# A four-stage transformer kernel: gate/up as pairs of 64-row tiles, down products in batches of their own, transposes by DMA

## The chip, the cores and the metric

One core of one Trainium2 chip. The metric is the device time of one execution in microseconds; lower is better. The kernel before takes 1253.09 us (median of the 4 runs made beside the changed kernel).

## The reference

Two layers, each a linear attention block with softmax feature maps and then a gated product (GLU), with residuals. S = 2048 tokens, D = 576, 32 heads of 18, F = 4608, bf16. Both layers use the same weights.

```python
qkv = x @ wqkv                                   # q, k, v per head
pq, pk = q @ w_phi, k @ w_phi                    # per head, 18 x 18
phi_q = concat([softmax(pq), softmax(-pq)]);  phi_k = likewise
kv = phi_k^T v;  z = sum over tokens of phi_k
attn = (phi_q kv) / (phi_q z + 1e-6) @ wo
glu  = ((x @ w_gate) * (x @ w_up)) @ w_down      # no nonlinearity
x = x + attn(layernorm(x)); x = x + glu(layernorm(x)); x = x + attn(layernorm(x)); x = x + glu(layernorm(x))
```

All K and V of a layer must be done before its first Q can be finished (kv is a sum over all tokens). That makes two places in which little else can run: the start, and the middle between the layers.

## The kernel before

The program is written as Python threads (`t_load`, `t_ln`, `t_ain` for K and V, `t_aout` for Q, `t_bmain` for the GLU, `t_wd` for the ring of down weights). A list scheduler orders their operations by modelled durations and emits one instruction stream per engine. The order is thus itself a product of the change: moving one operation can reorder others.

In the GLU, the 576 rows of the contraction are four full K tiles of 128 and one of 64. Gate and up each take five matmuls per step of 128 of the 4608 columns, the fifth with a zero half; the down product of a step follows two steps later, so both kinds interleave all through.

```python
for k in range(5):                       # gate
    lhsT = Wg[:, k, fs] if k < 4 else Wr[:, fs]
    ops.append(... matmul(ps[:, gub, 0:256], lhsT, xT[:, k, tok], ...))
for k in range(5):                       # up; the half row is read from xT[:, 5]
    lhsT = Wu[:, k, fs] if k < 4 else Wr[:, fs]
    ops.append(... matmul(ps[:, gub, 256:512], lhsT, xT[:, k if k < 4 else 5, tok], ...))
...                                      # two steps later: 2 x (512 + 64) columns of the down product
    ps[:, bank, 0:512] += hT . wdr[:, slot, fi, 0:512];  ps[:, Z, ...] += hT . wdr[:, slot, fi, 512:576]
```

The gate, up and attention weights stay on chip. The down weights (5.3 MB) do not fit and are streamed again for every block of 256 tokens, through a ring of three slots of 432 KB (`NWD = 3`, `CH = 3`: three steps to a piece). Every load is issued from SyncE. The layer norm's output is transposed on TensorE:

```python
ops.append(Op(60, lambda e: e.transpose(pT[:, 128*k:128*k+128], xln[:, sl[j], 128*k:128*k+128], s.ident[:])))
... act: copy(xT[:, 0:5, tok], pT)
```

## Time and profile before

| | before |
|---|---|
| median | 1253.09 us (1250.22 to 1254.75) |
| PE busy, share of span | 96% |
| first gate matmul | 125.25 us |
| one GLU step, gate/up and down | 1.09 + 0.49 us |
| down weights | 192 pieces of 432 KB, 3.3 us to land (median) |

How to read it: a PE at 96% leaves only PE work and the two attention-bound places to gain from.

### The profile page before, as it was taken

Reading aid. Unit: us, or ns where it says so; the run is one execution under the profiler, and the core shown is the slowest. Engines: PE = TensorE matmul, PEld = TensorE weight load, DVE = VectorE, ACT = ScalarE, POOL = GpSimd, SP = SyncE. Lnnn points to the kernel's source line nnn. Section 1 sums busy time; section 2 is a strip of 40 time slices with the busy share of each in tenths; the row PEclk is TensorE's granted clock in tenths of the full one; section 3 lists DMA queues with packets and bytes.
Section 4 is the critical chain, followed back from the end, with each engine's and each line's share of the span. In section 5 each row is a group of like instructions: output and inputs, shape, how many; then the busy total and the mean of one; then the engine's idle time right before and its main releaser. Section 6 shows DMA issues by size and latency. Waiting matters only on the chain.

```text
span 1250.4 us, 25739 instructions
## 1 busy us (share of the span) xinstructions
PE 1198.8 (96%) x11096; PEld 936.1 (75%) x11096; DVE 619.3 (50%) x1478; ACT 546.4 (44%) x1393; POOL 272.5 (22%) x268
## 2 busy tenths in 40 slices
PE   6796999999999999999999889999999999999998
PEld 4574777778787777777767568778777777777776
DVE  6898646445553323323269974455445332323232
ACT  7887545445353323222258765444444322222222
POOL 4796212112120000000039742112112000000000
PEclk9998999999999999999999889999999999999999
DMA  9700122222222333333320002222222233323232
GB/s 316 230 2 1 41 75 72 74 85 72 85 73 86 88 99 89 98 90 97 94 64 2 1 2 73 86 82 74 82 84 82 86 97 99 105 91 110 87 109 67
DMA packets 85832, 104.61 MB, mean 84 GB/s; under 512 B 4374, under 2 KB 84566, under 8 KB 84566
## 3 DMA queue, kind: packets, MB, share of 16 engines
q1 hardware_dynamic: 85718, 102.96, 27.0%
q8 instruction: 87, 1.43, 0.5%
q14 instruction: 27, 0.22, 0.1%
HBM read 100.59 MB, written 2.36 MB: 82 GB/s over the span
## 4 chain that ended last, share of the span: by engine, by line
PE 84%; DVE 6%; POOL 5%; ACT 4%; issue 0%; DMA 0%; SPq 0%; DVEq 0%
PE ps L1071 25%; PE ps L1076 25%; PE ps L1109 20%; PE ps L808 4%; PE ps L1019 3%; POOL dd L869 3%; PE ps L1112 3%; DVE ss L855 2%; PE ps L946 2%; POOL dd L833 1%; PE ps L965 1%; PE ps L783 1%; DVE dd L841 1%; PE ps L998 1%; DVE mxmn L823 1%; DVE mxmn L828 1%
## 5 line engine op out<-in xcount | busy, mean ns | idle before, releaser
L1086 DVE TENSOR_TENSOR hT<-ps,gsb 128x256 bf16<-128x256 f32 x576 | 243.9, 423 | 577.2 <-ACT gsb L1084 575.9
L1084 ACT CAST gsb<-ps 128x256 bf16<-128x256 f32 x576 | 214.2, 372 | 621.7 <-PE ps L1076 585.3
L1109 PE MATMUL ps<-wdr,hT 128*128 128x512 bf16 x1152 | 357.5, 379 | 0.4 <-DVE x_sb L1135 0.4
L1071 PE MATMUL ps<-xT,Wg 128*128 128x256 bf16 x2304 | 347.2, 273 | 0.0
L1076 PE MATMUL ps<-xT,Wu 128*128 128x256 bf16 x2304 | 346.1, 273 | 0.0
L1071 PEld LDWEIGHTS ps<-xT,Wg 128*128 128x128 bf16 x2304 | 187.2, 98 | 80.8
L1076 PEld LDWEIGHTS ps<-xT,Wu 128*128 128x128 bf16 x2304 | 225.7, 98 | 26.4
L1112 PE MATMUL ps<-wdr,hT 128*128 128x64 bf16 x1152 | 221.9, 193 | 0.5 <-DVE x_sb L1138 0.5
L869 POOL TENSOR_TENSOR dd<-dd,rr 128x576 bf16<-128x576 bf16 x128 | 146.1, 1163 | 121.1 <-ACT rr L863 121.1
L1109 PEld LDWEIGHTS ps<-wdr,hT 128*128 128x128 bf16 x1152 | 112.6, 98 | 76.8 <-DVE x_sb L1135 0.7
L1071 PE MATMUL ps<-xT,Wr 128*128 128x256 bf16 x576 | 157.2, 273 | 0.0
L1076 PE MATMUL ps<-xT,Wr 128*128 128x256 bf16 x576 | 157.2, 273 | 0.0
L772 POOL TENSOR_SCALAR xln<-x_sb,nmean,rstd 128x576 bf16<-128x576 bf16 x64 | 51.9, 821 | 367.1 <-ACT rstd L767 366.9
L833 POOL TENSOR_TENSOR dd<-psb,mxmn 128x576 bf16<-128x576 bf16 x64 | 74.4, 1163 | 231.6 <-DVE mxmn L823 231.6
L1112 PEld LDWEIGHTS ps<-wdr,hT 128*128 128x128 bf16 x1152 | 112.7, 98 | 6.5 <-DVE x_sb L1138 0.8
L855 DVE TENSOR_REDUCE ss<-dd 128x64 f32<-128x1152 bf16 x64 | 86.4, 1350 | 22.8 <-ACT dd L850 22.5
L1071 PEld LDWEIGHTS ps<-xT,Wr 128*128 128x128 bf16 x576 | 56.5, 98 | 6.6
L1076 PEld LDWEIGHTS ps<-xT,Wr 128*128 128x128 bf16 x576 | 56.4, 98 | 6.6
L820 ACT CAST psb<-ps 128x288 bf16<-128x288 f32 x128 | 47.9, 400 | 17.3 <-PE ps L808 15.3
L949 ACT COPY eT<-ps 108x768 bf16<-108x768 bf16 x64 | 50.8, 798 | 8.5 <-PE ps L965 4.9
L828 DVE TENSOR_REDUCE mxmn<-ps 128x16 f32<-128x288 f32 x128 | 52.0, 448 | 0.0
L841 DVE TENSOR_TENSOR dd<-ps,mxmn 128x288 bf16<-128x288 f32 x128 | 51.7, 447 | 0.0
(85 smaller groups left out, 1143.8 us busy)
## 6 DMA issues: line engine op xcount, KB each, us to landing
wdr<-in_B_w_down_dram SPq DMA_DIRECT2D x192, 432.0 KB, 3.3
Wg<-in_B_w_gate_dram SPq DMA_DIRECT2D x4, 1152.0 KB, 12.3
Wu<-in_B_w_up_dram SPq DMA_DIRECT2D x4, 1152.0 KB, 27.3
x_sb<-in_A_x_dram SPq DMA_DIRECT2D x4, 576.0 KB, 5.8
out_dram<-x_sb SPq DMA_DIRECT2D x8, 288.0 KB, 3.7
Wraw<-in_A_wqkv_dram SPq DMA_DIRECT2D x8, 144.0 KB, 4.8
Wv<-in_A_wqkv_dram SPq DMA_DIRECT2D x1, 576.0 KB, 3.9
Wo<-in_A_wo_dram SPq DMA_DIRECT2D x1, 576.0 KB, 6.6
```

What stands on the lines that cost most here:

```text
L772: ops.append(Op(800, (lambda e, j=j: e.tensor_scalar(xln[:, sl[j], 0:576], x_sb[:, ss[j], :], nm[:, sl[j]:sl[j] + 1], rstd[:, sl[j]:sl[j] ...
L828: ops.append(Op(370, (lambda e, h=h, pv=pv: e.tensor_reduce(mxmn[:, pz, 1, 16 * h:16 * h + 16], pv, AX.X, ALU.min)), reads=[("pbd", bank)] ...
L833: yield ("ops", "pool", [Op(1170, (lambda e: e.tensor_tensor(d1, p3, mxb, ALU.subtract)), reads=[("psb", pz, 0), ("psb", pz, 1), ("mx", pz ...
L841: ops.append(Op(370, (lambda e, d2h=d2h, pv=pv, mnbh=mnbh: e.tensor_tensor(d2h, pv, mnbh, ALU.subtract)), reads=[("pbd", bank), ("mn", pz, ...
L855: Op(1320, (lambda e: e.tensor_reduce(ss[:, sm, :].rearrange("p (b g) -> p b g", b=2), e4, AX.X, ALU.add)), reads=s.ddk(sm, 0) + s.ddk(sm, ...
L869: yield ("ops", "pool", [Op(1150, (lambda e, ev=ev, rb=rb: e.tensor_tensor(ev, ev, rb, ALU.mult)), reads=s.ddk(sm, br) + [("rr", sm), ("dd ...
L1071: ops.append(Op(d_pe(256), (lambda e, lhsT=lhsT, rhs=rhs, k=k, gub=gub: e.matmul(ps[:, gub, 0:256], lhsT, rhs, start=(k == 0), stop=(k == ...
L1076: ops.append(Op(d_pe(256), (lambda e, lhsT=lhsT, rhs=rhs, k=k, gub=gub: e.matmul(ps[:, gub, 256:512], lhsT, rhs, start=(k == 0), stop=(k = ...
L1084: yield ("ops", "act", [Op(372, (lambda e, g=g, gub=gub: e.copy(gsb[:, g, :], ps[:, gub, 0:256])), reads=[("GUg", gub)], writes=[("gsb", g ...
L1086: yield ("ops", "dve", [Op(425, (lambda e, g=g, h=h, gub=gub: e.tensor_tensor(hT[:, h, :], ps[:, gub, 256:512], gsb[:, g, :], ALU.mult)), ...
L1109: ops.append(Op(d_pe(512), (lambda e, lhsT=lhsT, bank=bank, slot=slot, fi=fi, f2=f2: e.matmul(ps[:, bank, 0:512], lhsT, s.wdr[:, slot, fi, ...
L1112: ops.append(Op(d_pe(64) + 6, (lambda e, lhsT=lhsT, sl=sl, slot=slot, fi=fi, f2=f2: e.matmul(ps[:, Z, 64 * sl:64 * sl + 64], lhsT, s.wdr[: ...
```

## The change

Its intent: save the wasted half of the fifth K tile, take the transposes off TensorE, and put work into the idle middle.

* Gate and up run as nine pairs of concurrent 64-row tiles per step. A `lock` keeps attention off TensorE for a gate/up batch of 36 steps (256 tokens).
* Then comes the down batch of those 36 steps, alone but for attention, which shares this phase.
* The K work of layer 2 is done under GLU 1, as far as its tokens are ready.
* Seven heads per attention tile instead of six (five overlapping tiles instead of six).
* The layer norm's output is transposed by DMA. These DMAs and the down weights are issued from SyncE; the loads of all other weights, and of x, move to ScalarE's queue.
* The ring of the down weights is four slots of 288 KB.

```diff
-CH = 3
+CH = 2
-        self.NPS, self.NSM, self.NVX, self.NET, self.NXP, self.NWD = 2, 4, 2, 3, 3, 3
+        self.NPS, self.NSM, self.NVX, self.NET, self.NXP, self.NWD, self.NG, self.NO = 2, 4, 2, 3, 2, 4, 2, 1
 # t_load
-                yield ("dma", g, emit, (), writes, nbytes, False)
+                yield ("dma", g, emit, (), writes, nbytes, False, False, 60.0, "act")
 # t_ln
-            yield ("ops", "pe", [... e.transpose(pT[...], xln[...], s.ident[:]) x 5 ...]) ; act copies
+            yield ("dma", s.g_xt[sl[j]], (lambda e: e.dma_start_transpose(xT[:, :, tok], xln[:, sl[j], :])), ...)
 # GLU (cut to its core)
+        def part(half, W, wk, which, tail):
+            r = slice(64 * half, 64 * half + 64)
+            ...
+                    seq = [(W[r, k, fs], s.xT[r, k, tok]) for k in range(4)]
+                    if tail:
+                        seq.append((s.Wr[r, fs], s.xT[r, 4, tok]))
+        lo = part(0, s.Wg, "Wg", 0, True) + part(0, s.Wu, "Wu", 1, False)
+        hi = part(1, s.Wu, "Wu", 1, True) + part(1, s.Wg, "Wg", 0, False)
+        for a_, b_ in zip(lo, hi):
+            ops += [a_, b_]
 ...
+            yield ("lock",)          # one gate/up batch
+            ...
+            yield ("unlock",)
+            yield ("go", s.t_down(L, b, on_block_done), 4, ...)   # 36 steps of the down product
```

## The prediction

> **What bounds the kernel now.** I read the page's busy row and its 40 slices first, then busy time by stretch, then the timeline of one steady GLU step, then the groups by shape.
>
> ```profile
> PE 1198.8 (96%) x11096; PEld 936.1 (75%) x11096; DVE 619.3 (50%) x1478; ACT 546.4 (44%) x1393; POOL 272.5 (22%) x268
> ...
> PE   6796999999999999999999889999999999999998
> ...
> DVE  6898646445553323323269974455445332323232
> ```
>
> TensorE (PE) is the bound in all but two places: the first four slices and the middle (slices 21 to 24), where VectorE (DVE) is full instead. Those are the attention K stages of layers 1 and 2. The table by stretch (PE, weight loads, DVE, ACT, POOL, granted clock, DMA share, GB/s) shows it:
>
> ```profile
> 0.00:125.00 125.00, 94.88 (x905) 71.12 (x906) 105.39 (x234) 100.46 (x254) 88.49 (x94) 0.95 0.42 137
> ...
> 145.00:640.00 495.00, 495.00 (x4595) 390.44 (x4593) 204.29 (x520) 181.58 (x472) 52.02 (x53) 1.00 0.29 86
> 640.00:732.00 92.00, 78.79 (x714) 57.96 (x713) 85.44 (x170) 74.15 (x188) 75.06 (x68) 0.93 0.02 6
> ...
> 750.00:1246.00 496.00, 494.81 (x4557) 389.20 (x4555) 194.16 (x482) 169.06 (x431) 43.04 (x42) 1.00 0.29 88
> ```
>
> Busy time of overlapped matmuls says little, so I need the distance between starts. One GLU step (128 of the 4608 columns, 256 tokens):
>
> ```profile
> 400.71 0.60 PE L1071 MATMUL ps<-xT,Wg 128*128 128x256 bf16 x4
> 401.15 0.27 PE L1071 MATMUL ps<-xT,Wr 128*128 128x256 bf16 x1
> 401.25 0.60 PE L1076 MATMUL ps<-xT,Wu 128*128 128x256 bf16 x4
> 401.69 0.27 PE L1076 MATMUL ps<-xT,Wr 128*128 128x256 bf16 x1
> 401.80 0.38 PE L1109 MATMUL ps<-wdr,hT 128*128 128x512 bf16 x1
> 402.02 0.19 PE L1112 MATMUL ps<-wdr,hT 128*128 128x64 bf16 x1
> 402.05 0.38 PE L1109 MATMUL ps<-wdr,hT 128*128 128x512 bf16 x1
> ```
>
> Ten 256-column matmuls take 401.80 - 400.71 = 1.09 us, 109 ns each; a 512 plus a 64 of the down product takes 0.245 us, so the down pair 0.49 us. A step is 1.58 us and there are 576, so the GLUs are 910 us of the 1250. In the same way the timeline gives 124 ns per 288-column matmul, 137 per 324, 57.5 per K-V outer product and 51 to 56 per transpose or attention output. Multiplied by the counts, all PE work is: gate/up 5760 x 109 = 628; down 576 x 0.49 = 282; Q, K and output projections 960 x 124 = 119; V 320 x 137 = 44; 864 transposes 48; K-V 22, attention output 20, weight fusion 6: 1169 us. The other 81 us of the span are PE idle or cold, about 45 of them before 125 us, 23 in the middle, the rest at the two ramps and the end.
>
> **What the Trainium skill says.** (1) "TensorEngine Tiling (Array Packing)", Key Properties: row tiles execute weight loads and matmuls in parallel; changing the tiling mode drains TensorE. Its Gotcha 1: two row tiles may not access one PSUM bank at once. The kernel before has no row tiles, so its trace cannot confirm this. The diff keeps the two tiles on different banks and swaps them half way through each group of four steps, with an ordering wait. (2) "TensorE: Matmul & The Clock Gate", Part 3, says that a weight load overlaps matmuls in flight only if its row group differs, and gives 3.07x for four 32-row tiles. The trace is better than the first half:
>
> ```profile
> 400.44 0.10 PEld L1109 LDWEIGHTS ps<-wdr,hT 128*128 128x128 bf16 x1
> 400.46 0.10 PEld L1112 LDWEIGHTS ps<-wdr,hT 128*128 128x128 bf16 x1
> ```
>
> full-array loads start 0.02 us apart while a matmul of the same rows runs. Two loads per 109 ns, which a tile pair needs, therefore look affordable. (3) "DMA: Bandwidth & Descriptors", Rules for kernel authors: transfers from several issuing queues share the same 16 engines. So the loads moved to ACT's queue will still interleave with the new transposes; in the first 50 us the trace has the DMA full (share 0.9 to 1.0).
>
> **The change, part by part.**
>
> *Gate/up.* 576 is 4.5 rows of 128. Before, the half row costs a whole zero-padded matmul for gate and another for up. After, nine 64-row halves of gate and nine of up run as nine concurrent pairs. If a pair costs what one full matmul costs (109), 576 x 9 x 109 = 565: 63 us less.
>
> *LN transposes to DMA.* 320 PE transposes x 56 ns go: 18 us of PE, and about 0.95 us of ACT per 128 tokens. Added: 64 DMA transposes of 160 KB, which lengthen each LN's latency by an estimated 3 us, hidden except in the start and the middle.
>
> *Seven heads per tile.* Per Q tile 10 instead of 12 transposes and outputs, per K tile 10 instead of 12 outer products; V 576 columns instead of 648. V 44 to 39, transposes of attention 30 to 27, K-V 22 to 19, output 20 to 19, fusion 6 to 5: 13 us less.
>
> PE work becomes 1169 - 63 - 18 - 13 = 1075 us. Mode switches: two per 256-token block, 32 in all; a drain is the 273 ns life of a matmul less its 109 ns slot, an estimated 0.16 us, so 5 us.
>
> *Where it is idle.* I rebuild the span by stage.
> (a) Start. DVE and POOL bind the K stage (3.42 us per tile in the timeline from 62 to 97 us), and that work stays. The K stage ended near 97.5; the first gate matmul came at 125 after two Q tiles. The new order lets the first gate/up batch start only when four Q tiles are done; before, the fourth was done near 138 us while sharing with GLU. I take 135.
> (b) GLU 1 from there: gate/up 8 x 35.3 = 282; down 8 x 17.6 = 141; twelve remaining Q tiles at 3.9 (10 x 124 for Q, as many for the output, 15 transposes, 10 outputs) = 47; fourteen K tiles of layer 2 at 3.0 = 42. Sum 512.
> (c) Middle: after the last down batch a serial chain. LN took 8.5 us before (x2 at 640 to xT at 648.5), plus 3 for the DMA; two K tiles 11.5 + 3.5; the K-V add and the barrier 6; then four Q tiles to x1, which took 42 us before (704 to 746) while the GLU had begun, here an estimated 33 alone. Sum 66 us, of which 22 are PE work. Before, 640 to 732 took 92 and the ramp lost 3 more.
> (d) GLU 2: 282 + 141 + 47 = 470. (e) End 5.
> Sum 135 + 512 + 66 + 470 + 5 = 1188; with switches 1193.
>
> *What a batch design can lose besides.* In a gate/up batch the pair of banks needed next must be emptied in 18 slots, 1.96 us; ACT (0.54, from 512 columns) then DVE (0.63), the matmul's tail and semaphores make about 1.6. One attention instruction in between, such as the 1.35 us DVE sum, eats the margin. I take 0.7 us per block, 11 us in all. Total 1204.
>
> ```profile
> L855 DVE TENSOR_REDUCE ss<-dd 128x64 f32<-128x1152 bf16 x64 | 86.4, 1350 | 22.8 <-ACT dd L850 22.5
> L828 DVE TENSOR_REDUCE mxmn<-ps 128x16 f32<-128x288 f32 x128 | 52.0, 448 | 0.0
> L841 DVE TENSOR_TENSOR dd<-ps,mxmn 128x288 bf16<-128x288 f32 x128 | 51.7, 447 | 0.0
> ...
> wdr<-in_B_w_down_dram SPq DMA_DIRECT2D x192, 432.0 KB, 3.3
> ```
>
> **The rivals.**
> R1, *the tiles are not really concurrent*. If half-row weight loads or the bank writes of two tiles collide, a pair could cost 130 to 150 ns instead of 109. Each 10 ns is 52 us. For it: skill's 3.07 of 4. Against it: the two load starts above. At 130 the total is near 1310.
> R2, *attention no longer fits the down phase*. The lock gives PE to gate/up for 35 us, so the two Q tiles of the next block must pass their chain (projection, maxima, exponentials, sums, normalising, transposes, output) within one down phase. Summing the durations of the groups for two tiles gives about 23 us; the phase has 17.6 + 7.8 = 25.4 us of PE work in layer 2, 31.5 in layer 1. For it: 2 us of slack only. If each of the twelve phases that hold Q tiles ran 4 us over, the total would be 1250.
> R3, *the down weights become the bound*. A batch reads 5.3 MB; 1.2 MB are prefetched, leaving 4.1 MB for 17.6 us, 235 GB/s, in phases with no attention, against 86 before. For it: 3.3 us to land a 432 KB piece. Against it: the start moves 316 GB/s, and only the last two blocks of GLU 2 and to a lesser degree of GLU 1 are so bare. About 4 to 8 us.
> R4, *the transposes starve the start*. With the loads full until 50 us, LN could wait for its transposes; the K stage would shift by 5 to 20 us.
>
> **Range and chances.** The stage sum with small losses is 1204. Perfect overlap gives 1193, and a shorter middle or start could take 20 more: 1170. R2 to R4 together, each at half its size, add some 40: 1245. R1 gets about 8%, and alone makes it slower. The 2% line is at 1229.0, a little less than one spread above 1204. I give 0.80 for faster by over 2%, 0.13 within, 0.07 slower.
>
> **What would show each step.** In the profile after: gate/up pairs at 108 to 112 ns from pair start to pair start (R1 if more); a gate/up batch of about 35 us without holes over 0.5 us (eviction margin); down phases of 31 us in layer 1 and 25 in layer 2 with PE full (R2 shows as PE waiting for POOL, ACT or DVE of attention before a gate/up batch; R3 as PE waiting for the down-weight DMA); first gate/up matmul at 130 to 140 us (R4 if later, with waits on the transposes); 60 to 72 us from the last down matmul of layer 1 to the first gate matmul of layer 2; and PE no longer bound by DVE from 640 to 732. I am wrong if the pair spacing or the waits before the gate/up batches are larger by a factor of two than stated.

## More of the kernel before

The experiments were run in three sets, on three chips; the kernel before, run again beside each set, had a median of 1252.3 us in all three, so times are also compared across sets.

One more view matters for what came: the last two rows of the 40 slices, the DMA engines' busy share (in tenths) and GB/s.

```profile
DMA  9700122222222333333320002222222233323232
GB/s 316 230 2 1 41 75 72 74 85 72 85 73 86 88 99 89 98 90 97 94 64 2 1 2 73 86 82 74 82 84 82 86 97 99 105 91 110 87 109 67
```

After the loads of the start, the DMA runs at 2 to 3 tenths throughout: the down weights flow evenly, because the down products are spread evenly.

## The result, and the profile after

The changed kernel takes 1257.91 us (1256.88 to 1258.87, 4 runs) against 1253.09 (4 runs). The ratio is 1.004, with a 95% interval of 1.0024 to 1.0056: the same, within 2%. The prediction of 1204 is wrong, and so is its range, by 13 us. Ratios here are the mean time of one kernel's fast runs over that of the other's of the same rounds, so they are not quite the ratio of the medians that are quoted.

The page's busy row and slices of the changed kernel:

```profile
PE 1125.3 (90%) x15104; PEld 853.9 (68%) x15172; DVE 591.9 (47%) x1243; ACT 438.0 (35%) x976; POOL 272.8 (22%) x271
...
PE   1377689999999999999999759999999999999998
...
DVE  3188775848653434343434475674832313122131
...
DMA  9820011514406061515151401240616060523414
GB/s 293 281 38 12 1 22 36 158 13 110 104 14 179 15 168 32 152 31 153 39 144 50 133 1 23 78 126 10 165 41 182 11 180 21 162 69 113 124 59 142
```

PE busy fell by 73.5 us, from 96% to 90% of the span: PE work did go (the prediction had 94 us, counted by the distance between starts and not by busy time). The first slices are worse (1, 3 where before were 6, 7), and the DMA row has changed its nature: zeros and sixes alternate. The transfers come in bursts.

Busy time by stretch (PE, weight loads, DVE, ACT, POOL, granted clock, DMA share, GB/s), cut at the first gate/up matmul, the last down matmul of layer 1, the first gate/up matmul of layer 2 and the last down matmul:

```profile
0.00:171.00 171.00, 95.35 (x780) 69.05 (x780) 105.48 (x241) 82.31 (x220) 86.67 (x93) 0.95 0.41 117
171.00:705.80 534.80, 522.03 (x7266) 400.06 (x7304) 265.53 (x537) 194.08 (x429) 114.46 (x109) 1.00 0.34 89
705.80:758.40 52.60, 29.89 (x236) 22.00 (x234) 33.74 (x88) 22.15 (x52) 21.66 (x22) 0.81 0.11 26
758.40:1251.00 492.60, 478.06 (x6825) 362.84 (x6856) 185.87 (x377) 139.48 (x276) 50.05 (x48) 1.00 0.34 95
```

Against the prediction's stage sum (135, 512, 66, 470, 5, and 16 for switches and stalls, which I put half to each GLU): the start is 36 us too long (171.2), GLU 1 is 15 (534.6 against 520) and GLU 2 is 15 too long (492.6 against 478), the middle is 13 too short (52.6), the end 1. Together 51 to 52: that is 1255.4, the span of the profiled run, less 1204.

**The gate/up batches.** The timeline of PE at the last pairs of the last batch, and the first weight load of the down batch that follows (start, duration, engine, line, operation, shape of tile and operands; in brackets the idle time before it):

```profile
1230.73 0.27 PE L1070 MATMUL ps<-xT,Wu 64*128 64x256 bf16 x1
1230.73 0.27 PE L1070 MATMUL ps<-xT,Wg 64*128 64x256 bf16 x1
1230.84 0.27 PE L1070 MATMUL ps<-xT,Wu 64*128 64x256 bf16 x1
1230.84 0.27 PE L1070 MATMUL ps<-xT,Wg 64*128 64x256 bf16 x1
...
1231.04 0.10 PEld L1137 LDWEIGHTS ps<-wdr,hT 128*128 128x128 bf16 x1 [0.21 <-issue]
```

Both tiles of a pair start together, 0.11 us apart from pair to pair. A batch of 324 pairs lasts 35.54 us in 13 of 16 cases. From the first start to the last it is 35.27 us for 323 distances: 109.2 ns.

At the switch a caution is due: 68 of the 1152 wide down matmuls have no record in this trace (the group below counts x1084), among them the first of this batch, so PE's next record, at 1231.27, is not the switch. The weight load above belongs to the missing matmul. In wd_once, an experiment below whose records are complete, the same place reads

```profile
1200.68 0.27 PE L1071 MATMUL ps<-xT,Wg 64*128 64x256 bf16 x1
1200.88 0.39 PE L1138 MATMUL ps<-wdr,hT 128*128 128x512 bf16 x1
```

The switch costs 0.20 us from start to start instead of 0.11.

**The down batches.** Of eight down phases in a layer, the first two are long (about 34 to 36 us from the first down matmul, in both layers) and hold all the remaining Q tiles but one, which ends in the third of layer 1. The other six run from 19.7 to 23.3 us, where 36 steps of 0.49 us would take 17.6. I call these six bare: in layer 2 they hold next to nothing else, in layer 1 two K tiles of layer 2 each (more in the last), most of it in the 5 us before the first down matmul. The last gate/up batch and the last down batch by stretch:

```profile
1195.60:1231.10 35.50, 35.50 (x650) 31.48 (x650) 12.59 (x21) 9.95 (x17) 0.00 (x0) 1.00 0.11 33
1231.30:1251.00 19.70, 18.86 (x141) 8.81 (x142) 1.25 (x3) 0.46 (x1) 0.00 (x0) 1.00 0.72 210
```

In the first the DMA is all but idle, since the ring is full and nothing is read from it. In the second it is the only other thing that runs. The groups of the down product and the row of the DMA issues:

```profile
L1137 PE MATMUL ps<-wdr,hT 128*128 128x512 bf16 x1084 | 293.6, 381 | 20.5 <-DMA wdr<-in_B_w_down_dram 19.7
...
L1137 PEld LDWEIGHTS ps<-wdr,hT 128*128 128x128 bf16 x1152 | 112.5, 98 | 161.3 <-DMA wdr<-in_B_w_down_dram 45.0
...
wdr<-in_B_w_down_dram SPq DMA_DIRECT2D x288, 288.0 KB, 3.3
```

After the bar is the idle time before the group's instructions, with what ended most of it. Before, the same matmul group waited 0.4 us in all, and for VectorE:

```profile
L1109 PE MATMUL ps<-wdr,hT 128*128 128x512 bf16 x1152 | 357.5, 379 | 0.4 <-DVE x_sb L1135 0.4
```

Now weight loads waited 45.0 us and matmuls 19.7 for the down weights (the two overlap, so they do not add). The chain that ended last says it too: before,

```profile
PE 84%; DVE 6%; POOL 5%; ACT 4%; issue 0%; DMA 0%; SPq 0%; DVEq 0%
```

and after, where 11 of the DMA's 13% are the down weights:

```profile
PE 74%; DMA 13%; DVE 5%; ACT 3%; POOL 2%; ACTq 1%; issue 1%; SPq 0%; DVEq 0%
```

**The start.** First ScalarE, in the timeline: its first work came at 12.47 us (2.1 us where it issues no loads, as the experiment late_sp shows), and then it stood again.

```profile
12.47 0.68 ACT L600 ACTIVATE Wraw<-Wraw 64x576 uint32<-64x576 uint32 x1 [10.38 <-issue]
...
20.64 1.29 ACT L691 COPY WT<-ps 126x640 bf16<-126x640 bf16 x2 [6.25 <-issue]
```

"issue" says that the engine waited for nothing that the profile shows; here ScalarE's own queue was busy in that time with DMA issues, some 0.5 us for each of over 30 loads. Then PE, with a hole from 27 to 44 us and another to 53:

```profile
44.34 1.74 PE L778 MATMUL ps<-Wv,xT 128*128 128x378 bf16 x5 [17.57 <-issue]
46.65 1.01 PE L778 MATMUL ps<-Wv,xT 128*128 128x198 bf16 x5 [0.57 <-ACT vx L857]
52.75 1.74 PE L778 MATMUL ps<-Wv,xT 128*128 128x378 bf16 x5 [5.10 <-DMA xT<-xln]
```

What these matmuls lacked is xT, the transposed tile: the last line says so, and in petr, where these transposes are not DMAs, the first such matmul comes at 29.44 us instead of 44.34. SyncE's timeline, the stretch from 30 to 40 us, and the line of the transposes' landing times:

```profile
24.44 31.96 SPq L764 DMA_TRANSPOSE xT<-xln  x6
```

```profile
30.00:40.00 10.00, 0.00 (x0) 0.00 (x0) 2.15 (x10) 0.00 (x0) 0.00 (x0) 1.00 1.01 410
```

```profile
DMA to landing us min/median/max: 2.6/2.9/26.8
```

Six transposes took SyncE 32 us to issue, and one took 26.8 us to land, while the DMA engines were full with the gate and up weights, at 410 GB/s. The first matmul that needs that load came at 171.2 us.

### The profile page after: what moved, and what is told of

Read it like the earlier page. It is cut to its first block, busy times and chain, and to the rows that moved or that the text cites. A ratio compares the mean times of both kernels' runs of the same rounds, so it can differ in the third digit from the quotient of the medians.

```text
span 1255.4 us, 33464 instructions
## 1 busy us (share of the span) xinstructions
PE 1125.3 (90%) x15104; PEld 853.9 (68%) x15172; DVE 591.9 (47%) x1243; ACT 438.0 (35%) x976; POOL 272.8 (22%) x271
## 2 busy tenths in 40 slices
DMA packets 130315, 115.61 MB, mean 92 GB/s; under 512 B 48892, under 2 KB 129020, under 8 KB 129020
## 4 chain that ended last, share of the span: by engine, by line
PE 74%; DMA 13%; DVE 5%; ACT 3%; POOL 2%; ACTq 1%; issue 1%; SPq 0%; DVEq 0%
PE ps L1070 45%; PE ps L1137 12%; DMA wdr<-in_B_w_down_dram 11%; PE ps L778 10%; DMA xT<-xln 3%; PE ps L1140 2%; POOL dd L839 2%; PE ps L964 1%; PE ps L981 1%; PE ps L867 1%; PE ps L1017 1%; DVE o L1006 1%; DVE ss L825 1%; DVE mxmn L793 1%; DVE mxmn L798 1%
## 5 line engine op out<-in xcount | busy, mean ns | idle before, releaser
L1070 PE MATMUL ps<-xT,Wg 64*128 64x256 bf16 x4608 | 568.0, 269 | 1.7 <-DMA xT<-xln 1.7
L1070 PE MATMUL ps<-xT,Wu 64*128 64x256 bf16 x4608 | 568.5, 269 | 0.9 <-DVE x_sb L1158 0.7
L1070 PEld LDWEIGHTS ps<-xT,Wg 64*128 64x128 bf16 x4608 | 429.5, 94 | 32.5 <-issue 2.9
L1070 PEld LDWEIGHTS ps<-xT,Wu 64*128 64x128 bf16 x4608 | 431.7, 94 | 28.7 <-DVE x_sb L1158 1.8
L1115 DVE TENSOR_TENSOR hT<-ps,gsb 128x512 bf16<-128x512 f32 x288 | 199.1, 691 | 341.7 <-ACT gsb L1113 341.3
L1113 ACT CAST gsb<-ps 128x512 bf16<-128x512 f32 x288 | 168.5, 585 | 543.9 <-PE ps L1070 543.3
L1137 PE MATMUL ps<-wdr,hT 128*128 128x512 bf16 x1084 | 293.6, 381 | 20.5 <-DMA wdr<-in_B_w_down_dram 19.7
L839 POOL TENSOR_TENSOR dd<-dd,ss 128x576 bf16<-128x576 bf16 x128 | 145.7, 1163 | 112.1 <-ACT ss L833 112.1
L1070 PE MATMUL ps<-xT,Wr 64*128 64x256 bf16 x1152 | 167.3, 269 | 0.0
L825 DVE TENSOR_REDUCE ss<-dd 128x64 f32<-128x1152 bf16 x64 | 85.2, 1341 | 19.7 <-ACT dd L820 19.5
L778 PE MATMUL ps<-Wv,xT 128*128 128x378 bf16 (+1 forms) x320 | 54.5, 306 | 26.1 <-issue 17.6
L1070 PEld LDWEIGHTS ps<-xT,Wr 64*128 64x128 bf16 x1152 | 65.3, 94 | 6.8
```

The lines of the kernel that those rows point to most:

```text
L778: ops.append(Op(d_pe(n), (lambda e, lhsT=lhsT, rhs=rhs, k=k: e.matmul(s.ps[:, bank, 0:n], lhsT, rhs, start=(k == 0), stop=(k == 4))), read ...
L825: Op(1320, (lambda e: e.tensor_reduce(ss[:, sm, :].rearrange("p (b g) -> p b g", b=2), e4, AX.X, ALU.add)), reads=s.ddk(sm, 0) + s.ddk(sm, ...
L839: yield ("ops", "pool", [Op(1150, (lambda e, ev=ev, rb=rb: e.tensor_tensor(ev, ev, rb, ALU.mult)), reads=s.ddk(sm, br) + [("ss", sm)], wri ...
L1070: out.append(Op(54.3, (lambda e, bank=bank, cs=cs, lhsT=lhsT, rhs=rhs, st=st, sp=sp: e.matmul(ps[:, bank, cs], lhsT, rhs, start=st, stop=s ...
L1113: yield ("ops", "act", [Op(540, (lambda e, g=g, gb=gb: e.copy(gsb[:, g, :], ps[:, gb, :])), reads=[("gu", gb)], writes=[("gsb", g)], excl= ...
L1115: yield ("ops", "dve", [Op(625, (lambda e, g=g, ub=ub, p=p: e.tensor_tensor(hT[:, p, :], ps[:, ub, :], gsb[:, g, :], ALU.mult)), reads=[(" ...
```

## The experiments

Two theories of the loss stood at the outset: A, the down weights bind the bare down batches; and C, the start is late because the gate and up weights stand in front of the transposes, and ScalarE issues them. The rest separates these and what is behind A: the size of the packets (E), the bytes under way (F), what the ring holds (G), or the cost of a piece (H).

### wd_once: the down weights fetched only once

```diff
-                yield ("dma", s.g_wd[slot], ...)
+                if (L, b) == (1, 0) and c < s.NWD:
+                    yield ("dma", s.g_wd[slot], ...)
```

The down products use stale weights on purpose. (The comparison with the reference still passes, so "correct" says nothing of this term.)

> The changed kernel, but the down weights are fetched only for the first four pieces and then read again from the same four slots: the result is wrong on purpose, the matmuls are the same. Theory A (the down weights bind the down batches: they came at 235 to 255 GB/s, a batch at full speed needs 288 KB per 0.98 us = 301 GB/s): the bare down batches of GLU 2 fall from 19.7 to 22.4 us to 17.6 to 17.9 us, the total falls by 35 to 42 us from 1257 to about 1218. Rival B (the batches wait for something else, the attention chain or the change of tile mode): the bare batches stay above 19.5 us and the total falls by less than 10 us.

Measured: 1225.02 us (1224.58 to 1226.49), ratio 0.9788 [0.977, 0.9806]. The last down batch, by stretch:

```profile
1200.90:1218.70 17.80, 17.79 (x146) 9.04 (x144) 1.49 (x3) 0.58 (x1) 0.00 (x0) 1.00 0.00 1
```

17.8 us instead of 19.7, PE full, DMA idle. The six bare batches of layer 2 take 107.5 us together instead of 125.0, those of layer 1 118.4 instead of 130.9. The first gate/up matmul stays at 171.8. Theory A holds, worth 33 us, a little under the 35 to 42 expected, and against the prediction nothing else in the GLU phases is left: from the first gate/up matmul to the last down matmul, without the middle, 520.3 + 473.3 = 993.6 us, where the prediction had 998.

### late_wgu: gate and up weights issued late

```diff
+        yield ("wait", ("ain", 1, 9))        # ten of sixteen K tiles are done
         yield from grp("wgu", items, "wloaded")
```

> The changed kernel with one wait more: the gate and up weights (10.4 MB) are issued half way through the K stage of layer 1 instead of at the start. Theory C (the first LN transposes stand behind the 9 KB packets of these weights in the DMA engines: landing took up to 26.8 us): the hole from 27 to 44 us goes, the first gate/up matmul moves from 171 us to 138 to 148 us, and the total falls by 25 to 33 us to about 1228. Rival D (ScalarE lost its time issuing the loads, about 0.5 us each): the ten loads cost 5 us wherever they stand, and the total falls by less than 7 us.

Measured: 1238.56 us (1237.44 to 1243.52), ratio 0.9907 [0.9878, 0.9937]; first gate/up matmul at 150.3. The loads were issued from 85 to 90 us, and the first four down pieces moved with them, from 0.8 to 75.7. SyncE's timeline and the landing times:

```profile
18.43 42.59 SPq L765 DMA_TRANSPOSE xT<-xln  x13
```

```profile
DMA to landing us min/median/max: 2.6/2.7/4.4
```

The collision is gone, and 21 us of the start with it. Theory C holds, though for less than the 25 to 33 us expected.

### petr: the first layer norm transposed on TensorE again

```diff
+            if sig[0] == "xT" and sig[1] == 1:
+                ... five e.transpose on PE, one copy on ACT ...
+                continue
             yield ("dma", s.g_xt[sl[j]], (lambda e: e.dma_start_transpose(...)), ...)
```

> The changed kernel with one part undone: the first LN of layer 1 (16 tiles) is transposed on TensorE again, the loads stay as the change has them. Theory C: no transpose then waits for DMA, the first gate/up matmul comes at 140 to 150 us instead of 171 us, total down by 20 to 30 us. Rival D: ScalarE is still held by the loads until 20 us, and has 16 copies of 0.69 us more: total unchanged within 5 us.

Measured: 1246.94 us (1242.82 to 1249.06), ratio 0.9957 [0.9928, 0.9986]. The first gate/up matmul came at 152.1, as in late_wgu, though the loads were early: so it is the meeting of transposes and loads that costs some 20 us, and taking away either one mends it. In the whole only 11 us of the 20 to 30 expected remained. The first down phase, which shares PE with Q tiles, took 42.4 us instead of 36.2: six of the 19 us went there. Why the schedule put it so was not tested.

### paired: longer runs in the down weights' descriptors

```diff
-fs = slice(128 * f, 128 * f + 128)
+fs = slice(128 * CH * (f // CH) + f % CH, 128 * CH * (f // CH + 1), CH)
-wdv = s.wd.rearrange("(f p) d -> p f d", p=128)
+wdv = s.wd.rearrange("(c p i) d -> p c i d", p=128, i=CH)
```

Each partition now reads 2304 contiguous bytes instead of two runs of 1152; to match, the columns of the gate and up weights are taken with a stride of two.

> The changed kernel, with neighbouring rows of w_down in one partition, so that a down piece is read in runs of 2304 bytes instead of 1152; gate and up take every second column for a weight load. Theory E (the engines lose a fixed time per packet, so the rate depends on the run's length: 9 KB packets of the start moved at 420 to 435 GB/s): the bare down batches fall to 17.7 to 19 us, total down by 25 to 38 us. Rival F (the four-slot ring and its 3.3 us from issue to landing is the limit): less than 8 us. Rival G (a weight load with stride two is slower): a pair takes more than 112 ns and each 10 ns cost 52 us.

Measured: 1257.59 us (1254.16 to 1260.72), ratio 1.0046 [1.0019, 1.0072]. The page's count of packets fell from 130315 to 93450, so the longer runs were real, but the bare down batches stayed at 20 to 21 us. Theory E falls. As a by-product: the pairs still started 109.2 ns apart, so the strided weight loads cost nothing.

### ring5: five slots instead of four

```diff
-... self.NWD ... = 2, 4, 2, 3, 2, 4, 2, 1
+... self.NWD ... = 2, 4, 2, 3, 2, 5, 2, 1
-        self.lnv = A("lnv", [128, 2 * self.NXP], F32)
-        self.rstd = A("rstd", [128, 2 * self.NXP], F32)
+        self.rstd = self.lnv = A("rstd", [128, 2 * self.NXP], F32)     # makes room
```

> Five slots of 288 KB in the ring of the down weights instead of four (one 32-byte tile is aliased to make room), nothing else. Theory F (the pieces in flight bound the rate: a slot comes free only when all its matmuls have read it, so three pieces or 0.86 MB are under way for 3.3 us each, about 260 GB/s): four under way should give about 350 GB/s while a down batch runs alone; the bare down batches (19.7 to 23 us after the change) fall to 17.6 to 18.5 and the time by 20 to 33 us, to 1225 to 1238. Rival G (the DMA engines themselves give no more than about 260 GB/s for this pattern): the bare down batches gain only the 0.3 MB more that is on chip when they begin, about 1 us each, and the time falls by under 14 us.

Measured: 1233.01 us (1232.82 to 1233.98), ratio 0.9847 [0.9832, 0.9862]: theory F's range. The bare batches of layer 2 but its first take 17.9 to 19.1 us, and the waits of the same two groups fell to

```profile
L1136 PE MATMUL ps<-wdr,hT 128*128 128x512 bf16 x1084 | 285.0, 380 | 5.2 <-DMA wdr<-in_B_w_down_dram 5.0
...
L1136 PEld LDWEIGHTS ps<-wdr,hT 128*128 128x128 bf16 x1152 | 112.7, 98 | 134.7 <-DMA wdr<-in_B_w_down_dram 9.4
```

The rate inside one bare batch, in stretches of 2 us, first of the changed kernel (from 6 us after the batch's start), then of ring5:

```profile
1181.37:1183.37 2.00, 1.95 (x18) 1.05 (x18) 0.00 (x0) 0.00 (x0) 0.00 (x0) 1.00 0.73 203
1183.37:1185.37 2.00, 1.73 (x15) 0.65 (x13) 0.00 (x0) 0.00 (x0) 0.00 (x0) 1.00 0.90 284
1185.37:1187.37 2.00, 1.75 (x13) 0.83 (x14) 0.00 (x0) 0.00 (x0) 0.00 (x0) 1.00 0.91 255
1187.37:1189.37 2.00, 2.00 (x18) 1.01 (x16) 0.00 (x0) 0.00 (x0) 0.00 (x0) 1.00 0.76 220
```

```profile
1161.42:1163.42 2.00, 1.95 (x18) 1.02 (x17) 0.00 (x0) 0.00 (x0) 0.00 (x0) 1.00 0.95 298
1163.42:1165.42 2.00, 1.81 (x17) 0.82 (x14) 0.00 (x0) 0.00 (x0) 0.00 (x0) 1.00 0.94 288
1165.42:1167.42 2.00, 2.00 (x17) 1.05 (x18) 0.00 (x0) 0.00 (x0) 0.00 (x0) 1.00 0.99 309
1167.42:1169.42 2.00, 1.95 (x18) 1.02 (x17) 0.00 (x0) 0.00 (x0) 0.00 (x0) 1.00 0.95 285
```

In the last two columns the engines are 73 to 91% busy at 203 to 284 GB/s with four slots, and 94 to 99% busy at 285 to 309 with five. So 255 GB/s was no limit of the engines: with more pieces under way they moved more. The expected 350 GB/s did not come, and could not, since PE reads a step of 147,456 bytes in 0.489 us, 302 GB/s. The engines are nearly full at that rate, too, so no run here tells how much more they could have given.

### ring1x9: nine slots of 144 KB

```diff
-CH = 2
+CH = 1
-... self.NWD = 4
+... self.NWD = 9
```

> Nine slots of 144 KB instead of four of 288 KB: 1296 KB of ring instead of 1152, of which eight pieces, 1.15 MB, may be under way instead of 0.86. Theory F (bytes in flight): close to what five slots of 288 KB give, a fall of 15 to 33 us. Rival H (each piece costs a fixed time at the queue, issue and completion): twice as many pieces, 576, so the bare down batches stay at 20 us or grow, and the time is the same or longer.

Measured: 1233.84 us (1231.96 to 1234.66), ratio 0.985 [0.9835, 0.9865]. Twice as many pieces, the same gain: rival H falls. A piece of half the size still takes 3.0 us to land (median), so what counts is how many bytes share those 3 us.

### ring3x3: three slots of 432 KB

```diff
-CH = 2
+CH = 3
-... self.NWD = 4
+... self.NWD = 3
```

> Three slots of 432 KB: the same 1296 KB of ring as nine slots of 144 KB (which gave 1233.8), but only two pieces, 0.86 MB, may be under way while the third is read, as many bytes as in the changed kernel. Theory F (what is in flight counts, not what the ring holds): the bare down batches stay at 20 to 23 us, 240 to 265 GB/s, and the time at 1248 to 1260. Rival G (what counts is only how much is on chip when the batch begins): as nine slots of 144 KB, 1230 to 1240.

Measured: 1282.5 us (1280.98 to 1284.9), ratio 1.0244 [1.022, 1.0268]. The ring holds exactly as much as ring1x9's, and the two are 49 us apart: rival G falls. Theory F had the direction right but expected the changed kernel's time, and it is 25 us longer. What was missed: the bigger piece also takes longer to land. The matmul group's wait and the row of issues:

```profile
L1137 PE MATMUL ps<-wdr,hT 128*128 128x512 bf16 x1152 | 307.2, 381 | 38.7 <-DMA wdr<-in_B_w_down_dram 38.3
...
wdr<-in_B_w_down_dram SPq DMA_DIRECT2D x192, 432.0 KB, 4.1
```

With the measured landing times one rule puts all four rings on the right side of the demand; it was made after the runs. Bytes under way are the ring less the slot being read, divided by the median landing time; the demand is 302 GB/s:

| ring | under way | lands in | estimated supply | measured time |
|---|---|---|---|---|
| 3 x 432 KB | 0.88 MB | 4.1 us | 216 GB/s | 1282.5 us |
| 4 x 288 KB (the change) | 0.88 MB | 3.3 us | 268 GB/s | 1257.9 us |
| 5 x 288 KB | 1.18 MB | 3.4 us | 347 GB/s | 1233.0 us |
| 9 x 144 KB | 1.18 MB | 3.0 us | 393 GB/s | 1233.8 us |

The supply column is an estimate from the columns before it (2 x 442,368 bytes by 4.1 us, and so on). Where it is above the demand, the wait is nearly gone. It is good for that side only, not as a rate: inside one bare batch ring3x3 moved 237 GB/s (1201.82 to 1215.20 us), not 216, and the engines were 94 to 99% busy at 285 to 309 GB/s in ring5, so the 347 and 393 were not reached. The landing time is itself no constant of the piece (144 KB took 3.0 us with nine slots and 3.2 in allsp1x10 with ten). The kernel before had the worst of these rings, and never felt it, because its down products were spread out.

### late_sp: the small loads off ScalarE, too

```diff
-                yield ("dma", g, emit, (), writes, nbytes, False, False, 60.0, "act")
+                yield ("dma", g, emit, (), writes, nbytes, False, False, 60.0, queue)   # "sp"; "act" for gate/up, late
```

> As late_wgu (the gate and up weights issued only after ten of the sixteen first K tiles), and besides all the other weight loads go from SyncE's queue instead of ScalarE's. The theory that issuing loads costs ScalarE its first 8 us or so: the first ScalarE work falls from 12 us back toward 2 to 4, the first gate matmul from late_wgu's 150.3 to about 141 to 145, and the time from 1238.6 to 1229 to 1234. The rival (the transposes of xln stand behind the loads on the SyncE queue, so they only start later): first gate matmul at 150 or later, no gain over late_wgu.

Measured: 1236.89 us (1234.5 to 1237.35), ratio 0.9873 [0.9858, 0.9888]; first gate/up matmul at 149.3. ScalarE did start at 2.08 us, but only 1 us of that reached the first gate/up matmul: the expectation of 141 to 145 failed, and what came is close to the rival's, 150 or later and no gain over late_wgu. The trace shows the rival at work. SyncE issued the small loads until 14.6 us, its first transpose only then, and this one landed after 7.7 us; the first K matmul came no earlier than in late_wgu (22.06 us, there of V):

```profile
22.39 1.38 PE L779 MATMUL ps<-Wk,xT 128*128 128x288 bf16 x5 [9.44 <-DMA xT<-xln]
```

ScalarE's timeline shows another thing that remained, in the middle of the K stage:

```profile
88.37 0.48 ACT L858 CAST vx<-ps 128x378 bf16<-128x378 f32 x1 [5.67 <-issue]
```

ten late gate and up loads, issued by the engine that the K stage needs.

### combo5: ring5 and late_sp together

> The edits of ring5 and of late_sp together. If the two losses are separate (the start, and the down weights), the gains add: 1195 to 1215, clearly faster than the kernel before. If what is won at the start is lost again later, as with the transposes on TensorE, it stays above 1220.

Measured: 1209.77 us (1208.07 to 1211.16), ratio 0.9656 [0.9639, 0.9672]. The two losses are separate, and their gains add, to some 3 us: ring5's ratio is 1.5% and late_sp's 1.3% below that of before, and the changed kernel's 0.4% above it, so that the two save 1.9 and 1.7 points; 1.004 less both is 0.968.

### allsp5: all loads from SyncE

```diff
-grp("wgu", items, "wloaded", "act")
+grp("wgu", items, "wloaded")          # SyncE, still after ("ain", 1, 9)
```

> combo5 (late gate/up loads, small loads on SyncE's queue, five slots) with the late gate and up loads issued from SyncE as well, so that ScalarE issues none. In combo5's twin late_sp ScalarE stood still 5.7 us at 82 to 88 us for ten issues in the middle of the K stage, which its work bounds through VectorE and GpSimd. If ScalarE's issuing is what is left of the late start: the first gate matmul from 149.7 to 141 to 145, and the time from 1209.8 to 1200 to 1206. If the K stage is slow for another reason: 1208 to 1212.

Measured: 1206.84 us (1205.51 to 1209.37), ratio 0.9639 [0.9618, 0.9659]. The first gate/up matmul moved from 149.7 to 143.5, inside the expectation, while the time, 2.9 us less, missed its range by under 1 us and lies at the edge of combo5's interval. For the first gate/up matmul, ScalarE's ten issues cost 6 us.

### allsp5_petr: and the first transposes on TensorE

> allsp5 with the first layer norm's tiles of layer 1 transposed on TensorE again. If the transposing DMAs still cost the start something when no gate/up load stands beside them: the first gate matmul falls another 5 to 12 us, to 130 to 138. If they do not: within 3 us of allsp5. In the time the gain may be eaten again by up to 8 us as in petr.

Measured: 1204.56 us (1203.27 to 1207.17), ratio 0.9621 [0.9601, 0.964]; first gate/up matmul at 139.8. The gain of 3.7 us is within neither expectation quite, nearer to "nothing". The edit did one thing more than was meant: the wait for ten K tiles only orders the program, and with no transposes before them in SyncE's queue the gate and up loads went out at 14.9 to 19.7 us, not at 76 to 81 as in allsp5. With the transposes on TensorE that did no visible harm. Nor does the 3.7 us price the transposing DMAs alone: in allsp5 the first four stand beside the small loads and land after 8.2 to 3.5 us, later ones after 2.6. The time cannot be told from allsp5's.

### allsp1x10: ten slots of 144 KB

> allsp5 with ten slots of 144 KB instead of five of 288 KB: the same 1440 KB, but nine pieces or 1.3 MB may be under way instead of 1.15. Theory F: the bare down batches, 17.6 to 19 us in combo5, come to 17.6 to 18.2, up to 8 us less in all. Rival: the engines' own rate of about 300 GB/s already bounds them, within 3 us of allsp5.

Measured: 1202.73 us (1202.18 to 1203.81), ratio 0.9604 [0.9588, 0.9621], the lowest median of all and 4% faster than the kernel before. It is 4 us below allsp5, between the two expectations. Its first gate/up matmul came at 146.8, 3.3 us later than in allsp5, though only the ring differs: a change of the start of some 3 us, read from one profile each, is thus no firm finding. PE at the down matmuls waited 3.3 us in all for the down weights. Its stretches, cut at the same events:

```profile
0.00:147.00 147.00, 97.79 (x816) 71.59 (x818) 109.83 (x253) 88.18 (x232) 91.14 (x97) 0.92 0.48 138
147.00:667.00 520.00, 518.02 (x7266) 398.03 (x7260) 260.90 (x525) 188.03 (x416) 108.54 (x104) 1.00 0.35 91
667.00:719.60 52.60, 30.33 (x242) 22.02 (x244) 33.40 (x88) 22.48 (x52) 23.07 (x23) 0.81 0.11 26
719.60:1197.30 477.70, 474.38 (x6856) 363.63 (x6856) 185.72 (x377) 139.64 (x276) 50.04 (x48) 1.00 0.34 97
```

PE is busy 518 of 520 us in GLU 1 and 474 of 478 in GLU 2.

## Why the prediction was wrong

| stage, us | predicted | changed kernel | wd_once | allsp1x10 |
|---|---|---|---|---|
| start, to the first gate/up matmul | 135 | 171.2 | 171.8 | 146.8 |
| GLU 1 (with half of the 16) | 520 | 534.6 | 520.3 | 520.1 |
| middle | 66 | 52.6 | 53.3 | 52.7 |
| GLU 2 (with half of the 16) | 478 | 492.6 | 473.3 | 477.7 |
| end | 5 | 4.4 | 4.6 | 4.8 |
| span | 1204 | 1255.4 | 1223.3 | 1202.1 |

* **Gate/up at the price of one matmul per pair: right.** Predicted 109 ns, measured 109.2. R1 is refuted. A step of gate/up takes 9 x 109.2 = 983 ns where it took ten such slots: 63 us over 576 steps, as predicted.
* **R2, attention does not fit the down phases: wrong.** The remaining Q tiles, all but one, went through in the first two down phases of each layer, of about 36 us with PE full. The prediction had them spread two to a phase.
* **Switches and eviction stalls, 5 + 11 us: the sum was too high.** A switch into the down batch costs 0.20 less 0.11, about 0.1 us; back from it, the first pair starts 0.12 us after a narrow down matmul whose own slot is 0.03, again about 0.1. The 32 switches come to some 3 us, where 0.16 each was predicted. Only three gate/up batches have a hole, of 0.3, 0.8 and 0.3 us: 1.4 us of stalls in all. So some 11 of the 16 us were not there. In wd_once, without the down weights' waits, the GLUs still took 12 us more than 512 + 470, so some 7 us lie in other terms of the sum, which were not taken apart.
* **R3, the down weights: the mechanism was right, the term was mis-sized.** I gave it "about 4 to 8 us" as a rival, and nothing in the stage sum. wd_once says 33. Two steps failed. First, "only the last two blocks of GLU 2 and to a lesser degree of GLU 1 are so bare": six of eight were in each layer (in layer 1 but for two K tiles each), since the first two down phases took nearly all the Q work. Second, "235 GB/s ... Against it: the start moves 316 GB/s": that is a mean over a batch, set against the rate of big loads all in flight together. What binds is the rate at which PE empties slots, 302 GB/s, against the bytes that the ring can have under way per landing time, an estimated 268 GB/s. The numbers were all in the profile of before: a step of 0.49 us, a landing time of 3.3 us, and a ring whose slots are freed only when read.
* **R4, the transposes starve the start: the mechanism was right, the term was mis-sized.** "The K stage would shift by 5 to 20 us" as a rival, none of it in the 135. The start is 36 us longer. Measured by what moved the first gate/up matmul: transposes behind the gate and up loads about 20 us (late_wgu 21, petr 19); moving the small loads' issues to SyncE 1 us (late_sp), since the transposes then stood behind them; the late ten issues on ScalarE 6 us (allsp5); the first transposes beside the small loads 3.7 us (allsp5_petr), which is hardly more than the 3.3 us by which the start of allsp5 and allsp1x10 differ. The prediction counted the ScalarE time that the change takes away, and never the issue time that it adds.
* **What is left of the start:** 139.8 us in the best case against 135, about 5 us. In allsp5_petr's K stage (24 to 113 us) VectorE waited 12.6 us for ScalarE's casts and exponentials, 8.1 of them once, at 84 us, for a layer norm that had come late; in the kernel before (20 to 98 us) 5.3. That fits a less regular order of the scheduler's, or the two pairs of layer norm buffers (`NXP`) where there were three; no run isolates either.
* **The middle, 66 us: too long by 13.** The later K work in GLU 1 did what it should. The trace of the changed kernel shows the terms: to the first K matmul (714.10) 8.3 us against 11.5; the two K tiles and their K-V products (to 732.06) 18.0 against 15; to the first attention output (735.13) 3.1 against 6; from there, the four Q tiles to the first gate/up matmul, 23.3 against 33. The Q tiles were the term that was too big.

So both large misses were in the list of rivals, each named with its mechanism and each given too little. With the two mended, the kernel comes to 1202.7 us. That this is the predicted 1204 is partly luck: there the start is still 12 us longer than in the stage sum and the middle 13 shorter. Only the two GLU stages agree on their own, and in them the 11 us too many for switches and stalls made up for what other terms lacked.

## What to carry to other kernels

Work that is regrouped into batches regroups its transfers as well: a stream that averages 85 GB/s may have to run at 300 in a third of the time and stand still in the rest. Size the ring from the burst: bytes under way (all slots less the one being read) over the measured landing time must exceed the rate at which the engine empties slots, and smaller pieces reach that in the same memory. And before small, urgent transfers are put on the DMA engines, look at what big and unhurried load stands there at that moment; issue the load later, and from an engine that has nothing else to do.

## What the Trainium skill lacked or had wrong

* "DMA: Bandwidth & Descriptors", Rules for kernel authors, says that a transpose next to ordinary DMAs "needs nothing". That is about correctness, and all runs were correct; about time nothing is said. Here a transpose of 160 KB landed in 2.7 us alone (median, late_wgu) and in up to 26.8 us beside gate and up loads at 410 GB/s, at a cost of about 20 us.
* "DMA: Bandwidth & Descriptors", section Bandwidth, has the rule to batch DMAs to at least 1 MiB for 75% of peak. The runs do not contradict it, but for a stream through a ring of fixed size it misleads: in the same 1296 KB, pieces of 144 KB with eight under way gave 1233.8 us (281 GB/s in a bare batch, from 1215.70 to 1224.30 us), pieces of 432 KB with two under way 1282.5 us (237 GB/s). No page has the rule of bytes under way by landing time.
* The same page, "Issuing engines are not separate DMA queues", calls the issuing time usually small beside the DMA. On an engine that also computes it was not: over 30 issues of about 0.5 us held ScalarE's first work back to 12.5 us and then stopped it for another 6.25; ten issues in the K stage stopped it for 5.67 (late_sp) and cost the start some 6 us (allsp5).
* "TensorEngine Tiling (Array Packing)", Key Properties, says that a change of mode drains TensorE, without a figure. Here it was about 0.1 us from pairs of 64-row tiles to full tiles (starts 0.20 us apart instead of 0.11, wd_once), and about as much the other way.
* No page has a rate for two 64-row tiles kept up with new weights for each matmul: 109.2 ns per pair of 256 columns for 35.5 us on end, the time of one full-array matmul before. Weight columns read with a stride of two cost nothing (paired).
